# Gated linear attention and two MoE layers: the scan keeps its floor itself, layer 1's first two blocks take turns at the features, one more buffer for the scan's loads

## The chip, the cores and the metric

One core of a Trainium2 chip. The time is device microseconds of one execution, the median of several runs; the profile is one execution of its own, with its own time. Engines: PE (TensorE, matmuls), PEld (its weight loads), DVE (VectorE), ACT (ScalarE), POOL (GpSimd), SP (SyncE, here the queue that issues all DMAs).

## The reference

```python
# batch 4, heads 8, sequence 768, head size 48
for t in range(S):
    state = alpha[:, :, t, :, None] * state + einsum('bhd,bhe->bhde', k[:, :, t], v[:, :, t])
    y[:, :, t] = einsum('bhd,bhde->bhe', q[:, :, t], state)
x = y as (3072 tokens, 384)
# layer 1: w_in 384 x 2048, w_out 2048 x 384, coefficients a (4) and b (2)
h = x @ w_in
g = (a0 + a1 h + a2 h^2 + a3 h^3) / (1 + |b0||h| + |b1| h^2 + 1e-6)
x = g @ w_out
# layer 2, same shapes
h = x @ w_in
out = (h * cos(h)) @ w_out
```

The decays alpha lie between 0.8 and 1. The weights of both layers come as 64-bit floats.

## The kernel before

Everything is scheduled by hand: the order of the instructions in the code is the order in which each engine runs its own, and an engine that waits holds back all that stands behind it.

**The scan.** The sequence is cut into 6 chunks of 128 steps, and a unit u is one chunk of one batch entry (24 units; 8 heads as 4 pairs, 48 of each 64 partitions in use). Slots n run from -3 to 24, and in each the engines work on several units at once (`attention`, L395). For a unit, DVE forms the running products p of the decays by one scan instruction (`decay`, L239, scan at L246: product so far times the next decay, plus `fresh`, a PSUM bank of zeros that holds the first decay in each head's first column). DVE then clips p from below at 2^-60 into the PSUM tile r with its sum in `chk` (`guess1`, L257, instruction at L261), ACT takes the logarithm and the exponential of its negative, again with a sum (`guess2`, L265, L268 and L269), and a Newton step on DVE makes the exact inverse (L276 and L284). POOL multiplies k by it (L288) and q by p (L293). PE forms the scores (L301), ACT copies them out (L308), POOL masks them (L313), PE adds the part from the state (L364) and from the scores (L374), transposes k (L321) and forms the update of the state (L333), which DVE applies (L345, L347); L254 is the last decay of a unit. In slot n: scores and masks copied for unit n, q and k scaled for n+1, guess for n+2, decay for n+3, state update for n-2, output of n-1.

**Its loads.** At the head of slot n, SP issues a for unit n+4 (two DMAs of 96.8 KB, L223), kq for n+2 (512 KB), v for n+1 (192 KB), the store of the output of n-2 (two DMAs of 96 KB, L391), then the fetch of one or two raw weight tiles (384 KB each, L143). There are 2 tiles for a, 4 for kq, 3 for v, used in turn. x of block 0 is read back in slots 8 to 10.

**Weights.** Layer 1 has 16 groups of 128 features (called features here), each with one tile of w_in (s = 0) and one of w_out (s = 1): 32 tiles, ordered by `w_order` (w_in tile i at place i, w_out tile i at i + 4). `w_fetch` (L131) loads a raw tile into a piece of the `spare` tile or a `raw` buffer; at most six are pending. `tick` (L155) runs the next of three conversion steps: ACT's L66 and L67, DVE's L71, DVE's L72. The low words go into the PSUM bank `words_t` in slots under 20 and into the tile itself behind that. `w_hi` (L175, ACT's L182) and `w_lo` (L185, L191 on POOL) split the result into two 32-bit parts. In the scan a step runs only while more than three tiles are pending.

**The layers.** From slot 20 on one iteration of `layers` (L623) stands behind each slot, and behind the last slot iterations alone: 96 per layer, of 6 blocks of 512 tokens x 16 features, in blocks' order. Iteration n issues `gemm1` (L469, nine matmuls at L478) of feature n into one of three banks, the element-wise work of the last four features (`rational`, L523, for layer 1: L536 to L557 and L516, L521), and `gemm2` (L482, nine matmuls at L491) of the feature five iterations back, which accumulates a block's 16 features in three PSUM banks. `acc_out` (L499) copies finished banks by ACT and stores them. Two `w_fetch` and two steps run in each of the iterations 4 to 15 of layer 1; from 16 on one of each, now for layer 2, whose w_in tiles go to DRAM until they are needed. x of the next block is loaded at feature 8 and split at 11, 12 and 13 (L599 on ACT, L603 on DVE). Iterations 16 and 18 sum up `chk` (L608, L615), and a flag chooses a general path if a sum is out of bounds.

Of the kernel before, what the change touches and what calls it, by code (L numbers as in the profile page):

```python
# [23 lines left out]
NU = NC * B  # L24
NO = 0
# [13 lines left out]
def attn_then_two_moe(ctx, tc, kqT, aT, vP, w1i, w1o, ma, mb, w2i, w2o, out):  # L39
# [56 lines left out]
    def bank(tag, shape=(128, TB), dtype=F32):  # L96
# [8 lines left out]
    chk = const.tile([128, 3, NU + 1], F32, name="chk")  # L105
    a_t = [const.tile([128, HP * (C + 1)], F32, name=f"a{i}") for i in range(2)]
    kq_t = [const.tile([128, 2, HP, C], F32, name=f"kq{i}") for i in range(4)]
    v_t = [const.tile([128, H * D + 64 - D], F32, name=f"v{i}") for i in range(3)]
# [19 lines left out]
    def in_spare(i):  # L128
        return i < 24 and i % 6 < 4
# [55 lines left out]
    def w_lo(engs):  # L185
        engs = list(engs)
        while to_lo:
# [6 lines left out]
            engs.append(engs.pop(0))  # L194
            if at is not None:
# [3 lines left out]
    def w_load(at):  # L199
        nc.sync.dma_start(out=ws[at // NF][at % NF].bitcast(F32), in_=wd[at])  # L200
# [38 lines left out]
    def decay(u):  # L239
# [4 lines left out]
        for hs in parts(u):  # L244
            nc.vector.tensor_tensor(out=fresh[:, hs, 0:1], in0=first[:, hs], in1=fresh[:, hs, 1:2], op=ALU.add)
            nc.vector.tensor_tensor_scan(  # L246
                d["p"][:, hs].rearrange("p a b -> p (a b)"), rest[:, hs].rearrange("p a b -> p (a b)"),
                fresh[:, hs].rearrange("p a b -> p (a b)"), 0.0, ALU.mult, ALU.add,
            )

    def last_decay(u):
        d = U[u]
        d["pc"] = in_p.tile([128, HP, 1], F32, tag="pc", name="pc", bufs=6)
        nc.vector.tensor_tensor(out=d["pc"], in0=d["p"][:, :, C - 1:], in1=fresh[:, :, 1:2], op=ALU.add)  # L254
# [661 lines left out]
```

## Time and profile before

| | |
|---|---|
| median of 3 runs | 965.47 us (962.27 to 965.59) |
| profiled execution, its own time | 963.49 us |
| its span, first to last instruction | 961.7 us |
| PE busy | 925.4 us, 96% |
| DVE, ACT, POOL busy | 668.8, 654.2, 612.2 us |
| DMA | 84.54 MB, 63.09 read from HBM, 20.45 written |

The span is what the trace covers; the execution's own time is 1.8 us longer. Busy time is an average over stages: the scan (to about 130 us), the last slots with layer 1's first iterations, then the layers alone. TensorE runs at one of two levels, 1.2 or 2.4 GHz, and a granted clock of 0.68 over a stretch means a mixture of the two.

### The profile page before, as it was taken

How to read it: one execution, taken by the hardware profiler on the slowest of the kernel's cores; microseconds unless marked ns; L12 is line 12 of the kernel's file. 1: busy time of each engine (PE TensorE's matmuls, PEld its weight loads, DVE VectorE, ACT ScalarE, POOL GpSimd, SP SyncE). 2: the span in 40 equal slices, each digit the busy share in tenths (PEclk: the TensorE clock that was granted, in tenths of full speed). 3: DMA queues.
4: the chain of work that ended last, by engine and by line, in shares of the span. 5: the costliest groups of instructions: out<-in, count | busy, mean ns of one | idle time of the engine just before them, and what ended most of it. 6: DMA issues, size and time to landing. Idle time of an engine off the chain costs nothing.

```text
span 961.7 us, 14225 instructions
## 1 busy us (share of the span) xinstructions
PE 925.4 (96%) x4976; PEld 745.8 (78%) x4976; DVE 668.8 (70%) x1089; ACT 654.2 (68%) x1196; POOL 612.2 (64%) x559
## 2 busy tenths in 40 slices
PE   7788799999999999999999999999999999999997
PEld 6677677778888888888888888888888888888885
DVE  8989889999999998989979956434334334343331
ACT  5888888878888878888777877554444444454442
POOL 4888899978998889989878755423232332333232
PEclk7988999999999999999999999999999999999999
DMA  7999853202213114022044233010100100100001
GB/s 230 316 299 286 262 184 87 89 2 91 74 58 124 33 51 131 33 100 82 33 140 157 83 121 109 1 66 1 35 32 1 66 1 1 66 1 1 33 1 36
DMA packets 47008, 84.54 MB, mean 88 GB/s; under 512 B 5521, under 2 KB 22161, under 8 KB 46929
## 3 DMA queue, kind: packets, MB, share of 16 engines
q1 hardware_dynamic: 46928, 83.55, 27.2%
q8 instruction: 41, 0.67, 0.3%
q14 instruction: 39, 0.31, 0.1%
HBM read 63.09 MB, written 20.45 MB: 87 GB/s over the span
## 4 chain that ended last, share of the span: by engine, by line
PE 80%; DVE 10%; DMA 4%; issue 2%; POOL 2%; ACT 1%; SPq 0%; DVEq 0%; ACTq 0%; POOLq 0%
PE acc L491 39%; PE b L478 38%; DMA v<-vP 2%; DVE p L246 1%; DVE st L72 1%; DMA spare<-w1o 1%; DVE z L536 1%; DVE g L552 1%; DVE r L541 1%; DVE g L539 1%; DVE z L284 1%; POOL kq L288 1%; DMA a<-aT 1%; DVE ah L276 1%; PE sc L301 1%
## 5 line engine op out<-in xcount | busy, mean ns | idle before, releaser
L521 POOL TENSOR_TENSOR lo<-g,hi 128x512 fp32r<-128x512 f32 x192 | 257.7, 1342 | 299.4 <-ACT hi L516 292.9
L478 PE MATMUL b<-x,w 128*128 128x512 f32 x1728 | 435.3, 396 | 3.7 <-DVE g L539 3.7
L491 PE MATMUL acc<-hi,w 128*128 128x512 f32 x1152 | 392.6, 396 | 0.0
L478 PEld LDWEIGHTS b<-x,w 128*128 128x128 f32 x1728 | 323.9, 188 | 84.2 <-DVE g L539 6.2
L491 PEld LDWEIGHTS acc<-hi,w 128*128 128x128 f32 x1152 | 216.5, 188 | 52.3
L516 ACT ACTIVATE hi<-g 128x512 fp32r<-128x512 f32 x192 | 121.3, 632 | 185.4 <-PE acc L491 118.9
L491 PE MATMUL acc<-lo,w 128*128 128x512 f32 x576 | 227.8, 395 | 0.0
L568 DVE TENSOR_TENSOR g<-ah,b 128x512 f32<-128x512 f32 x96 | 65.7, 684 | 140.3 <-ACT ah L566 140.3
L547 POOL TENSOR_TENSOR z<-z,ah 128x512 f32<-128x512 f32 x96 | 124.9, 1301 | 8.0
L491 PEld LDWEIGHTS acc<-lo,w 128*128 128x128 f32 x576 | 108.3, 188 | 26.1
L78 DVE SCALAR_TENSOR_TENSOR ah<-z,b 128x512 f32<-128x512 int32 x96 | 65.7, 684 | 37.6 <-ACT z L77 37.6
L77 ACT ACTIVATE z<-b 128x512 int32<-128x512 f32 x96 | 57.0, 594 | 50.1 <-PE b L478 50.1
L548 DVE TENSOR_TENSOR g<-g,b 128x512 f32<-128x512 f32 x96 | 65.1, 678 | 24.7 <-ACT g L545 24.5
L546 POOL TENSOR_SCALAR z<-ah,cq 128x512 f32<-128x512 f32 x96 | 75.2, 783 | 1.6 <-ACT ah L544 1.6
L545 ACT ACTIVATE g<-b,cq 128x512 f32<-128x512 f32 x96 | 74.6, 777 | 0.0
L552 DVE SCALAR_TENSOR_TENSOR g<-g,cq,r 128x512 f32<-128x512 f32 x96 | 70.7, 737 | 0.1
L539 DVE SCALAR_TENSOR_TENSOR g<-g,cq,b 128x512 f32<-128x512 f32 x96 | 70.5, 735 | 0.0
L566 ACT ACTIVATE ah<-ah,half_pi 128x512 f32<-128x512 f32 x96 | 68.1, 709 | 0.0
L556 ACT ACTIVATE r<-z,lnb 128x512 f32<-128x512 f32 x96 | 66.7, 695 | 0.0
L541 DVE SCALAR_TENSOR_TENSOR r<-z,r 128x512 f32<-128x512 f32 x96 | 65.4, 681 | 0.0
L536 DVE SCALAR_TENSOR_TENSOR z<-z,r 128x512 f32<-128x512 f32 x96 | 64.8, 675 | 0.3 <-ACT kq L182 0.3
L544 ACT ACTIVATE ah<-b 128x512 f32<-128x512 f32 x96 | 56.4, 588 | 6.5 <-PE b L478 6.4
(109 smaller groups left out, 987.6 us busy)
## 6 DMA issues: line engine op xcount, KB each, us to landing
kq<-kqT SPq DMA_DIRECT2D x24, 512.0 KB, 5.2
raw<-w2i SPq DMA_DIRECT2D x16, 384.0 KB, 3.1
raw<-w2o SPq DMA_DIRECT2D x16, 384.0 KB, 3.1
w<-wd SPq DMA_DIRECT2D x16, 384.0 KB, 3.1
v<-vP SPq DMA_DIRECT2D x24, 192.0 KB, 4.5
x<-x0d SPq DMA_DIRECT2D x18, 256.0 KB, 3.7
x1d<-o SPq DMA_DIRECT2D x18, 256.0 KB, 2.2
x<-x1d SPq DMA_DIRECT2D x18, 256.0 KB, 3.5
```

Source lines behind the costliest of these rows:

```text
L478: nc.tensor.matmul(h, ws[0][f][:, w, ks], x[:, xx, kk, :], start=i == 0, stop=i == 8)
L491: nc.tensor.matmul(acc[k], ws[1][f][:, w, ks], d[g], start=f == 0 and i == 0, stop=f == NF - 1 and i == 2)
L516: nc.scalar.activation(out=t["hi"], in_=t["g"], func=AF.Copy)
L521: eng.tensor_tensor(out=t["lo"], in0=t["g"], in1=t["hi"].bitcast(F32), op=ALU.subtract)
L536: nc.vector.scalar_tensor_tensor(z, z, ONE_EPS, r, ALU.add, ALU.mult)
L539: nc.vector.scalar_tensor_tensor(g, g, cq[:, 3:4], two["h"], ALU.add, ALU.mult)
L541: nc.vector.scalar_tensor_tensor(r, z, -2.0 / LN_S, r, ALU.add, ALU.mult)
L545: nc.scalar.activation(out=g, in_=h, func=AF.Identity, scale=cq[:, 5:6], bias=cq[:, 4:5])
L546: nc.gpsimd.tensor_scalar(zz, ah, cq[:, 1:2], cq[:, 0:1], ALU.mult, ALU.add)
L547: nc.gpsimd.tensor_tensor(out=zz, in0=zz, in1=ah, op=ALU.mult)
L552: nc.vector.scalar_tensor_tensor(g, g, cq[:, 2:3], r, ALU.add, ALU.mult)
L566: nc.scalar.activation(out=two["r"], in_=two["r"], func=AF.Sin, bias=half_pi)
```

## The change

- The scan takes the larger of product and `fresh`, and `fresh` is filled with 2^-60, so p never falls below it; `guess1` goes, and ACT's logarithm reads p. The sums move to the two Newton instructions (the first one now takes the smaller of p and 1e16, times r).
- Layer 1's blocks 0 and 1 take turns: features 0 to 9 of block 0, 0 to 9 of block 1, then 10 to 15 of block 0 and of block 1 (iterations 0, 10, 20 and 26 on). The first part's sums are copied by ACT into kq tiles and added by DVE at the end. x of block 1 is loaded at iteration 3 and split at 5 to 7; x of block 2 is loaded at iteration 26 and split at 28 to 30.
- The weights' order, the number fetched per slot (two in slots 0, 7 and 14 instead of in every fourth), and the steps in layer 1 (one per iteration from 3 to 31; layer 2's from 32) follow that.
- a has 3 tiles, kq 5, v 4, and each is loaded one slot earlier; the fetch of weights stands ahead of the output's store.

```diff
+H1 = 10
...
-    chk = const.tile([128, 3, NU + 1], F32, name="chk")
-    a_t = [const.tile([128, HP * (C + 1)], F32, name=f"a{i}") for i in range(2)]
-    kq_t = [const.tile([128, 2, HP, C], F32, name=f"kq{i}") for i in range(4)]
-    v_t = [const.tile([128, H * D + 64 - D], F32, name=f"v{i}") for i in range(3)]
+    chk = const.tile([128, 2, NU + 1], F32, name="chk")
+    a_t = [const.tile([128, HP * (C + 1)], F32, name=f"a{i}") for i in range(3)]
+    kq_t = [const.tile([128, 2, HP, C], F32, name=f"kq{i}") for i in range(5)]
+    v_t = [const.tile([128, H * D + 64 - D], F32, name=f"v{i}") for i in range(4)]
...
-        [(0, s, i) for i in range(NF) for s in range(2)], key=lambda w: (w[2] + 4 * w[1], w[1])
+        [(0, s, i) for i in range(NF) for s in range(2)],
+        key=lambda w: (w[2] + 5 * w[1] + (H1 if w[2] >= H1 else 0), w[1])
...
-        return i < 24 and i % 6 < 4
+        return i < 22 and i % 6 < 4
...
-            nc.vector.tensor_tensor(out=fresh[:, hs, 0:1], in0=first[:, hs], in1=fresh[:, hs, 1:2], op=ALU.add)
+            nc.vector.tensor_tensor(out=fresh[:, hs, 0:1], in0=first[:, hs], in1=fresh[:, hs, 1:2], op=ALU.max)
             nc.vector.tensor_tensor_scan(
...
-                fresh[:, hs].rearrange("p a b -> p (a b)"), 0.0, ALU.mult, ALU.add,
+                fresh[:, hs].rearrange("p a b -> p (a b)"), 0.0, ALU.mult, ALU.max,
...
-    def guess1(u):
+    def guess(u):
         d = U[u]
         d["r"] = bank("b1" if u == 1 else "r0", (128, HP, C))
         for hs in parts(u):
-            nc.vector.tensor_scalar(
-                d["r"][:, hs], d["p"][:, hs], P_MIN, None, ALU.max, ALU.add, accum_out=sums(1, u, hs)
-            )
-
-    def guess2(u):
-        for hs in parts(u):
-            r = U[u]["r"][:, hs]
-            nc.scalar.activation(out=r, in_=r, func=AF.Ln)
-            nc.scalar.activation(out=r, in_=r, func=AF.Exp, scale=-1.0, accum_out=sums(0, u, hs))
+            nc.scalar.activation(out=d["r"][:, hs], in_=d["p"][:, hs], func=AF.Ln)
+            nc.scalar.activation(out=d["r"][:, hs], in_=d["r"][:, hs], func=AF.Exp, scale=-1.0)
...
-            d["m"][:, hs], d["r"][:, hs], 1.0, d["p"][:, hs], ALU.mult, ALU.mult, accum_out=sums(2, u, hs)
+            d["m"][:, hs], d["p"][:, hs], RANGE, d["r"][:, hs], ALU.min, ALU.mult, accum_out=sums(1, u, hs)
...
-        nc.vector.scalar_tensor_tensor(d["n"][:, hs], d["m"][:, hs], -2.0, d["r"][:, hs], ALU.add, ALU.mult)
+        nc.vector.scalar_tensor_tensor(
+            d["n"][:, hs], d["m"][:, hs], -2.0, d["r"][:, hs], ALU.add, ALU.mult, accum_out=sums(0, u, hs)
+        )
...
     def where(n):
         m, r = divmod(n, N1)
+        if n < 2 * H1:
+            return 0, *divmod(n, H1)
+        if n < 2 * NF:
+            blk, f = divmod(n - 2 * H1, NF - H1)
+            return 0, blk, H1 + f
         return m, *divmod(r, NF)
+
+    def part(blk, k):
+
+        return kq_t[2 * blk + k // 2][:, k % 2].rearrange("p a b -> p (a b)")
...
+        first = f == 0 or in_parts(m, blk) and f == H1
+        last = f == NF - 1 or in_parts(m, blk) and f == H1 - 1
...
+            if f < NF - 1:
+                nc.scalar.activation(out=part(blk, k), in_=acc[k], func=AF.Copy)
+                continue
             o = in_p.tile([128, TB], F32, tag="p", name="o")
-            if m == 1 and k == 1:
+            if in_parts(m, blk):
+                nc.vector.tensor_tensor(out=o, in0=part(blk, k), in1=acc[k], op=ALU.add)
+            elif m == 1 and k == 1:
...
-        split = f in (11, 12, 13) and n < 2 * N1 and nxt[0] < 2
+        at, load = f - 11, f == 8
+        if n < NF:
+            nxt, at, load = (0, 1), n - 5, n == 3
+        elif n < 2 * NF:
+            at, load = f - 12, f == 10
+        split = 0 <= at < NK and n < 2 * N1 and nxt[0] < 2
...
-        if n < NF:
-            for _ in range(2):
+        if n < 2 * NF:
+            if n > 1:
                 w_fetch(2 * NF)
-            tick(0 if n < 4 else 2)
+                tick(1 if n > 2 else 0, 1)
...
-        nc.vector.memset(fresh, 0.0)
+        nc.vector.memset(fresh, P_MIN)
...
+            if n == -1:
+                load(3, "a")
+                load(1, "v")
             if n >= -1:
-                load(n + 4, "a")
+                load(n + 5, "a")
             if n >= 0:
-                if n:
-                    load(n + 2, "kq")
-                load(n + 1, "v")
+                load(n + 3, "kq")
+                load(n + 2, "v")
+                for i in range((min(n, 1) if n % 7 else 2) if n <= LEAD else 0):
+                    w_fetch(2 * NF)
                 if n >= 2:
                     y_store(n - 2)
-                for i in range(min(n, 1) if n % 4 else 2):
-                    w_fetch(2 * NF)
```

## Rows read from the trace of the kernel before

**Rows 1.** Windows by stage: busy us of each engine (instructions), granted clock, DMA share, GB/s
```profile
...
0.00:130.32 130.32, 104.69 (x1342) 87.39 (x1343) 115.23 (x279) 102.02 (x226) 101.02 (x123) 0.88 0.86 272
...
130.32:209.00 78.68, 74.88 (x442) 58.13 (x440) 75.68 (x108) 64.95 (x120) 75.00 (x66) 1.00 0.28 85
209.00:955.30 746.30, 745.82 (x3197) 600.28 (x3195) 477.89 (x704) 487.05 (x850) 436.22 (x371) 1.00 0.17 56
...
```

**Rows 2.** Waits of PE, 130.3 to 209 us: total us, times, longest us
```profile
...
PE b L478 <- DVE g L539: 3.7, 5, 1.5
```

**Rows 3.** Timeline of DVE, 15 to 130 us: start us, us, engine, line, operation
```profile
...
15.90 1.22 DVE L246 TENSOR_TENSOR_SCAN p<-a,r 128x512 f32<-128x512 f32 x1
...
38.03 1.22 DVE L246 TENSOR_TENSOR_SCAN p<-a,r 128x512 f32<-128x512 f32 x1
...
45.28 1.22 DVE L246 TENSOR_TENSOR_SCAN p<-a,r 128x512 f32<-128x512 f32 x1
...
55.31 1.22 DVE L246 TENSOR_TENSOR_SCAN p<-a,r 128x512 f32<-128x512 f32 x1
...
64.34 1.22 DVE L246 TENSOR_TENSOR_SCAN p<-a,r 128x512 f32<-128x512 f32 x1
...
68.43 0.69 DVE L261 TENSOR_SCALAR_CACHE_REDUCE r<-p 128x512 f32<-128x512 f32 x1
69.05 0.14 DVE L261 DVE_READ_ACCUMULATOR r<-p 128x1 f32 x1
...
69.36 1.22 DVE L246 TENSOR_TENSOR_SCAN p<-a,r 128x512 f32<-128x512 f32 x1
...
79.39 1.22 DVE L246 TENSOR_TENSOR_SCAN p<-a,r 128x512 f32<-128x512 f32 x1
...
87.37 1.22 DVE L246 TENSOR_TENSOR_SCAN p<-a,r 128x512 f32<-128x512 f32 x1
...
92.39 1.22 DVE L246 TENSOR_TENSOR_SCAN p<-a,r 128x512 f32<-128x512 f32 x1
...
104.35 1.22 DVE L246 TENSOR_TENSOR_SCAN p<-a,r 128x512 f32<-128x512 f32 x1
...
112.33 1.22 DVE L246 TENSOR_TENSOR_SCAN p<-a,r 128x512 f32<-128x512 f32 x1
...
122.36 1.22 DVE L246 TENSOR_TENSOR_SCAN p<-a,r 128x512 f32<-128x512 f32 x1
...
126.72 1.22 DVE L246 TENSOR_TENSOR_SCAN p<-a,r 128x512 f32<-128x512 f32 x1
...
```

**Rows 4.** The same view of windows for three single stretches of the scan
```profile
...
0.00:13.10 13.10, 6.76 (x39) 6.11 (x40) 9.94 (x26) 4.24 (x10) 3.80 (x19) 0.81 0.69 206
45.28:55.31 10.03, 8.10 (x88) 6.62 (x86) 9.69 (x24) 8.07 (x18) 9.69 (x12) 0.68 0.93 300
64.34:79.39 15.05, 11.41 (x182) 9.57 (x182) 14.53 (x36) 14.38 (x33) 14.33 (x16) 1.00 1.00 323
...
```

**Rows 5.** Chain of work that ended last, 28 to 145 us: start us, us, what
```profile
...
38.05 4.22 DMA v<-vP
...
81.82 0.51 ACT b L67
...
```

**Rows 6.** Groups of instructions, 64.3 to 79.4 us: busy us, mean ns, idle before
```profile
...
L288 POOL TENSOR_TENSOR kq<-kq,z 128x512 f32<-128x512 f32 x4 | 5.1, 1280 | 1.3 <-DVE z L284 1.3
...
L191 POOL TENSOR_TENSOR w<-st,w 128x384 fp32r<-128x384 f32 x4 | 4.0, 1001 | 0.0
...
L313 POOL TENSOR_SCALAR_AFFINE_SELECT lo<-lo 128x512 f32<-128x512 f32 x3 | 1.9, 636 | 0.0
...
```

**Rows 7.** Instructions of lines 71 and 72: count, duration ns min/median/max, first and last start
```profile
...
L71 DVE SCALAR_TENSOR_TENSOR st<-st,raw x32: 549/1479/1694, 129.6 to 563.3; 128x384 int32<-128x384 int32 x32
L71 DVE SCALAR_TENSOR_TENSOR b<-st,b x21: 539/552/599, 24.4 to 118.5; 128x384 int32<-128x384 int32 x21
...
L72 DVE SCALAR_TENSOR_TENSOR st<-raw,st x32: 544/798/1655, 130.2 to 563.9; 128x384 int32<-128x384 int32 x32
...
```

More of the change, by code (lines that the diff above doesn't have):

```diff
@@ L116, in attn_then_two_moe @@
     w_order = sorted(
-        [(0, s, i) for i in range(NF) for s in range(2)], key=lambda w: (w[2] + 4 * w[1], w[1])
+        [(0, s, i) for i in range(NF) for s in range(2)],
+        key=lambda w: (w[2] + 5 * w[1] + (H1 if w[2] >= H1 else 0), w[1])
     ) + [(1, s, i) for s in range(2) for i in range(NF)]
+    ready = set()
     spare = x_p.tile([128, 2, NK, TB], F32R, tag="x", name="spare").rearrange("p a b c -> p (a b c)").bitcast(I32)
@@ L194, in w_lo @@
             engs.append(engs.pop(0))
+            ready.add((m, s, i))
             if at is not None:
@@ L199, in w_load @@
     def w_load(at):
+        assert (1, at // NF, at % NF) in ready
         nc.sync.dma_start(out=ws[at // NF][at % NF].bitcast(F32), in_=wd[at])
@@ L253, in last_decay @@
         d["pc"] = in_p.tile([128, HP, 1], F32, tag="pc", name="pc", bufs=6)
-        nc.vector.tensor_tensor(out=d["pc"], in0=d["p"][:, :, C - 1:], in1=fresh[:, :, 1:2], op=ALU.add)
-    def guess1(u):
+        nc.vector.tensor_tensor(out=d["pc"], in0=d["p"][:, :, C - 1:], in1=fresh[:, :, 1:2], op=ALU.max)
+    def guess(u):
         d = U[u]
@@ L423, in attention @@
                 tick(0 if on(n + 2) else 1)
-        if n not in (-1, 0) and on(n + 2):
-            guess1(n + 2)
         tick(1)
@@ L428, in attention @@
             decay(n + 3)
-        if n in (-2, -1):
-            guess1(n + 3)
         tick(1)
@@ L440, in attention @@
         if n not in (-1, 0) and on(n + 2):
-            guess2(n + 2)
+            guess(n + 2)
         if n in (-2, -1):
-            guess2(n + 3)
+            guess(n + 3)
         if on(n - 1):
@@ L466, in where, with in_parts @@
         m, r = divmod(n, N1)
+        if n < 2 * H1:
[3 more added lines that the diff above has]
+            return 0, blk, H1 + f
         return m, *divmod(r, NF)
+    def in_parts(m, blk):
+        return m == 0 and blk < 2
+    def part(blk, k):
+        return kq_t[2 * blk + k // 2][:, k % 2].rearrange("p a b -> p (a b)")
     def gemm1(n):
         m, blk, f = where(n)
+        assert m or (0, 0, f) in ready
         h = bank(f"b{n % 3}")
@@ L484, in gemm2 @@
         d = T.pop(n)
+        assert m or (0, 1, f) in ready
+        first = f == 0 or in_parts(m, blk) and f == H1
+        last = f == NF - 1 or in_parts(m, blk) and f == H1 - 1
         for k in range(NK):
-            if f == 0:
+            if first:
                 acc_out()
@@ L491, in gemm2 @@
                 nc.tensor.matmul(
-                    acc[k], ws[1][f][:, w, ks], d[g], start=f == 0 and i == 0, stop=f == NF - 1 and i == 2
+                    acc[k], ws[1][f][:, w, ks], d[g], start=first and i == 0, stop=last and i == 2
                 )
-            if f == NF - 1:
-                outs.append((m, blk, k))
+            if last:
+                outs.append((m, blk, f, k))
     outs = []
@@ L603, in x_lo @@
         nc.vector.tensor_tensor(out=lo, in0=lo.bitcast(F32), in1=hi.bitcast(F32), op=ALU.subtract)
-    ok = const.tile([128, 3, NU], F32, name="ok")
+    ok = const.tile([128, 2, NU], F32, name="ok")
     def all_ok0():
         nc.vector.tensor_tensor(out=chk[:, :, 0], in0=chk[:, :, 0], in1=chk[:, :, NU], op=ALU.add)
-        nc.vector.tensor_scalar(ok[:, 0:2, :], chk[:, 0:2, :NU], RANGE, None, ALU.is_le)
-        nc.vector.tensor_scalar(ok[:, 2, :], chk[:, 2, :NU], -float(HP * C), None, ALU.add)
-        nc.vector.tensor_tensor(out=ok[:, 2, :], in0=ok[:, 2, :], in1=ok[:, 2, :], op=ALU.mult)
-        nc.vector.tensor_scalar(ok[:, 2, :], ok[:, 2, :], 0.0625, None, ALU.is_le)
+        nc.vector.tensor_scalar(ok[:, 0, :], chk[:, 0, :NU], -RANGE, None, ALU.is_ge)
+        nc.vector.tensor_scalar(ok[:, 1, :], chk[:, 1, :NU], -float(HP * C), None, ALU.add)
+        nc.vector.tensor_tensor(out=ok[:, 1, :], in0=ok[:, 1, :], in1=ok[:, 1, :], op=ALU.mult)
+        nc.vector.tensor_scalar(ok[:, 1, :], ok[:, 1, :], 0.0625, None, ALU.is_le)
     def all_ok1():
-        cnt = bank("r1", (1, 3 * NU))
+        cnt = bank("r1", (1, 2 * NU))
         nc.tensor.matmul(cnt, ones, ok.rearrange("p a b -> p (a b)"), start=True, stop=True)
@@ L641, in layers @@
         if split:
-            x_hi(*nxt, f - 11)
+            x_hi(*nxt, at)
         second(n)
-        if n < 2 * N1 and nxt[0] < 2 and f == 8:
+        if n < 2 * N1 and nxt[0] < 2 and load:
             for kk in range(NK):
```

6 lines of the change are left out of this document (3 added, 3 removed).

## Prediction, made before the change was run

> **What bounds the kernel now.** I read the stages first [rows 1]. From 209.00 us on, PE is busy 745.82 of 746.30 us: nothing is to be had there, and whatever reaches it earlier ends earlier by the same amount. Between 130.32 and 209.00 PE is busy 74.88 of 78.68 us and DVE 75.68. Up to 130.32, where PE starts layer 1's first feature, PE is busy only 104.69 us; so this change can win up to there, and some 3.8 us in the middle stage. The waits of that stage [rows 2] give the 3.7 us: PE waits five times for L539 of DVE, which frees a feature's bank.
>
> Then the scan itself. The start of DVE's scan instruction marks the slots [rows 3]: slot 0 at 15.90, slot 20 at 126.72, so 20 slots in 110.82 us, 5.54 each. They are not alike: 64.34 to 69.36 takes 5.02, and so does each of the two from there to 79.39. Six are longer: 38.03 to 45.28 is 7.25 (2.23 too long), 55.31 to 64.34 is 9.03 (4.01), 79.39 to 87.37 and 104.35 to 112.33 are 7.98 (2.96 each), and the two slots from 92.39 to 104.35 take 11.96 (1.92). Together 14.1 us over the level of 5.02.
>
> What sets that level stands in one row of windows [rows 4], 64.34 to 79.39, three slots: DVE 14.53, ACT 14.38, POOL 14.33 and PE 11.41 of 15.05 us, and the DMA engines 1.00 busy at 323 GB/s. DVE is the fullest engine, but ACT and POOL are 1% behind it and the DMA is full. What makes the long slots stands in the chain of waits [rows 5]: three loads of v stand in it one behind the other, the last at 38.05 with the long slot behind it. At 81.82 it is ACT's L67, which had to wait for DVE's L72: two weights are converted in that slot, they share one bank of low words, and ACT, in order, comes late to the logarithms on which DVE's next slot begins.
>
> **The change, part by part.** *The floor kept by the scan.* guess1 goes. One of them starts at 68.43 and its accumulator's read at 69.05, 0.62 us later; the read, 0.14 long, mostly lies under what follows, so I take 0.66 us of DVE per slot [rows 3]. In exchange L284 gets such a read: between nothing and 0.14; I take nothing, as the next operation after it needs no result of it. Max for add in the scan and min for mult in L276 are not in the trace. Nearest row: the scan with add, 1.22 us. I take the same; bounds are 0 and, were it to run like two instructions, 1.22 more a slot, which I leave out as nothing here points to it. ACT loses its read of an accumulator.
>
> In the run-in, three guesses of this size (two halves, two whole) lie ahead of slot 0, where DVE is the chain: 3 x 0.66 = 2.0 us earlier, bounds 1 and 3.
>
> In the slots DVE would fall from 5.02 to 4.36, but the others do not: POOL has per slot two multiplications of 1.28, two masks of 0.64 and one weight of 1.00, 4.84 summed [rows 6], some 4.65 as they overlap. The DMA moves per slot a 0.20, k and q 0.52, v 0.20, the output 0.20 and a weight 0.39 MB, 1.51 MB: at 323 GB/s 4.67 us [rows 4], at the 272 GB/s of the whole stage 5.55 [rows 1]. So the level lies between 4.67 and 5.55; I take 4.85, near the low end, since the row of 323 GB/s is of undisturbed slots. That is 0.17 x 14 slots = 2.4 us. The last slot, 122.36 to 126.72 [rows 3], takes 4.36 us because no weight is converted in it; now one is: 0.5 lost.
>
> *Loads ahead and buffers.* v, a and kq each get one more slot between release and need; the fetch of a weight now passes the output's store on SP's queue (the store's one reader, x's load, stands slots behind it: nothing). The first long slot, 2.23 us, is the v loads' and goes.
>
> *Two weights in one slot.* By the code before, two weights are fetched in slots 0, 4, 8, 12 and 16, and five steps run in slots 8, 12 and 16, four in the slot behind them. After, slots 0, 7 and 14 fetch two: two slots with five steps are left. I give each the 2.96 us of today. So of 14.1 us of excess 5.9 remain: 8.2 won. If the loads and DVE are not the cause but PE's low level (below), less goes: bounds 3 and 12.
>
> *The turns in layer 1.* Features 10 to 15 are needed only from iteration 20 on. Counting the fetches in the code, 24 weights are fetched by slot 20 in either kernel: the scan is hardly relieved. What is relieved is the middle stage: one step per iteration instead of two. Eleven conversions stood in it, about nine do now. In this form they have long and short rows, 549 to 1694 ns [rows 7]; at the medians, 1.48 + 0.80 = 2.28 us a weight, that is 4.6 us less on DVE in 78.68, against 3.0 us that it was idle [rows 1]. Of the 3.7 us that PE waits I count 2.5 as gone (bounds 0 and 3.7), because the three splits of x for block 1 come earlier into the same stretch, at iterations 5 to 7. The six copies of partial sums go to ACT, six adds to DVE in place of ACT copies at iterations 31 to 37, each about the 0.69 of L261, an instruction of the same size [rows 3]: the weights of layer 2 start only at 32, so DVE has room; nothing, and 6 x 0.69 = 4 us if that cover were gone. Layer 2's second weights are ready two iterations ahead of use instead of five: nothing, while DVE is busy only 477.89 of 746.30 us there [rows 1].
>
> The Trainium skill has a rule that speaks against this part: "GPSIMD Engine Reference" (section "Key points") says that GpSimd shares its SBUF interfaces with VectorE and contends with instructions of two SBUF inputs. [Rows 7] agree: 539 to 599 ns with one input in PSUM, up to 1694 without. By the rule alone, each of the eight conversions left under layer 1 would be a long one.
>
> *Sum:* 2.0 + 2.4 - 0.5 + 8.2 + 2.5 = 14.6 us off the profiled execution's own 963.49 us (span 961.7 and 1.8 around it): 948.9. The median of the runs shown is 965.47, 2.0 above it; I add half of that and say 950. As a check, PE would start layer 1 at 118.2: some 35.5 MB moved by 130.32 [rows 1] would need 110 us at 323 GB/s, so it can be had, with the DMA at 95%.
>
> **Rivals.** *The DMA keeps the slots.* If it gives 300 GB/s, as in 45.28 to 55.31 [rows 4], a slot takes 5.03 us: DVE's saving is idle time, and half of the excess stays as late loads. Then 2.0 - 0.5 + 4.1 + 2.5 = 8.1 us, 955.4, or 956 to 960 with less. For it: the full DMA of the best slots. Against: the first 13.10 us have it at 0.69 busy, and the extra buffers fill that.
>
> *Long conversions under layer 1.* If all eight take the 3.35 us of the two longest rows [rows 7] instead of 2.28, DVE has 8 x 1.07 = 9 us more; with the 3.0 idle and 4.6 relieved, PE waits some 2 us more than now instead of 2.5 less: 953 to 954. This is what the skill's rule above would make of it.
>
> *PE left at the low level: slower.* From 45.28 to 55.31 the granted clock averages 0.68 [rows 4], that is, 2.4 GHz for a part and 1.2 GHz for the rest; a slot's 3.80 us of PE work becomes 7.6, 2.75 over a slot of 4.85. If a faster DVE leaves PE in bursts with gaps while it waits for POOL and loads, in more slots than today, each costs 2.75: at five more the gain is gone, at nine it is 24.8 - 14.6 = 10 us slower, 974. For it: two such stretches stand in the scan now. Against: PE's share of a slot rises from 76 to 78%, and the gaps ahead of those stretches come with the long slots. "TensorE: Matmul & The Clock Gate" of the Trainium skill (Part 1) says that the throttled state is the default and activity releases it; the row agrees that the scan does not hold the clock, and no row tells which gap decides.
>
> *It doesn't do what it says.* If guess1's work was hidden behind POOL and the long slots stay as they are, only the run-in and part of the middle are left: 3 us, 961 to 963.
>
> **How the numbers follow.** Forecast (944 to 956) 0.60, of which 0.10 with the long conversions; DMA 0.20 (956 to 960.5); better than forecast, slots at the 4.67 of the DMA and no long ones, 0.05 (940 to 944); no effect 0.09; low level 0.06. A measurement can tell about 0.5%, 4.8 us, from no change. Faster by more: 0.85; within: 0.09; slower: 0.06. The range takes the forecast and the DMA case and the bounds of their terms: 941 to 960.
>
> **What would show it.** Right: no L261; scan starts 4.7 to 5.0 us apart with two long slots (7 and 14); slot 20 near 114 instead of 126.72; L478 first at 118; PE's waits for L539 under 2 us. Wrong: slots still at 5.02 with DVE idle ahead of L276 behind ACT or POOL; PE idle in front of the first feature of a turn (iterations 10, 20, 26, 32) or at iterations 100 to 111; more of the scan at the low clock.

## The result and the profile after

| | before | after |
|---|---|---|
| median of 4 runs | 963.87 us (961.43 to 965.59) | 949.20 us (947.75 to 950.29) |
| profiled execution, its own time | 963.49 us | 950.29 us |
| its span | 961.7 us | 948.5 us |

The ratio is 0.9848 (95% interval 0.9831 to 0.9866): 1.5% faster, 14.7 us. The forecast was 950.0 us in a range of 941 to 960. The total was met; the two terms of its sum on the scan's slots were not, and their errors nearly cancel, so that the total came right by luck as far as the scan goes. That is what the rest of this document is about.

First the page of the changed kernel, its span and its line of busy times. PE is now busy for 97% of the span; DVE has 16.7 us less to do, ACT and POOL 2.8 and 1.4.

```profile
span 948.5 us, 14172 instructions
...
PE 916.7 (97%) x4976; PEld 740.0 (78%) x4976; DVE 652.1 (69%) x1070; ACT 651.4 (69%) x1171; POOL 610.8 (64%) x560
...
```

The view of windows, with the changed kernel's own borders of the stages (columns as in [rows 1]: length, busy us of PE, PEld, DVE, ACT and POOL with their instructions, granted clock, DMA share, GB/s). The fourth line is the scan's slots alone, the last two are two of its long slots.

```profile
...
0.00:117.78 117.78, 96.63 (x1342) 81.23 (x1342) 102.81 (x251) 96.96 (x198) 97.66 (x121) 0.94 0.95 307
117.78:196.46 78.68, 76.15 (x450) 60.02 (x448) 70.80 (x108) 65.46 (x121) 72.45 (x66) 1.00 0.21 63
196.46:942.10 745.64, 743.89 (x3189) 598.75 (x3187) 478.46 (x713) 488.98 (x854) 440.68 (x374) 1.00 0.18 58
13.90:114.10 100.20, 85.05 (x1250) 70.77 (x1250) 88.56 (x216) 86.87 (x179) 90.63 (x98) 0.96 0.97 315
43.58:51.61 8.03, 8.03 (x90) 6.80 (x89) 5.33 (x14) 6.34 (x14) 5.49 (x7) 0.66 0.95 294
82.06:90.30 8.24, 6.78 (x100) 5.47 (x100) 5.93 (x15) 7.23 (x16) 5.92 (x7) 1.00 0.93 296
...
```

Against [rows 1], layer 1's first feature starts at 117.78 instead of 130.32, 12.54 us earlier. From there to PE's last matmul (at 939.96, before at 954.43) it takes 822.2 us instead of 824.1, 1.9 less, and what follows that last matmul takes 8.5 instead of 7.3. 12.5 + 1.9 - 1.2 = 13.2 us is the whole difference of the two profiled executions.

The timeline of DVE shows where the 12.5 us come from (start us, us, engine, line, operation). L251 is the scan instruction, and its starts mark the slots as in [rows 3].

```profile
...
13.80 1.22 DVE L251 TENSOR_TENSOR_SCAN p<-a,r 128x512 f32<-128x512 f32 x1
...
32.26 1.22 DVE L251 TENSOR_TENSOR_SCAN p<-a,r 128x512 f32<-128x512 f32 x1
...
34.64 3.18 DVE L736 TENSOR_SCALAR cq<-cab 128x4 f32<-128x4 f32 x1
...
39.33 1.22 DVE L251 TENSOR_TENSOR_SCAN p<-a,r 128x512 f32<-128x512 f32 x1
...
43.58 1.22 DVE L251 TENSOR_TENSOR_SCAN p<-a,r 128x512 f32<-128x512 f32 x1
...
49.53 0.69 DVE L275 SCALAR_TENSOR_TENSOR ah<-p,r 128x512 f32<-128x512 f32 x1 [1.54 <-ACT r L267]
...
51.61 1.22 DVE L251 TENSOR_TENSOR_SCAN p<-a,r 128x512 f32<-128x512 f32 x1
...
70.83 1.22 DVE L251 TENSOR_TENSOR_SCAN p<-a,r 128x512 f32<-128x512 f32 x1
...
73.97 2.33 DVE L621 TENSOR_TENSOR x<-x 128x512 fp32r<-128x512 f32 x1
...
77.82 1.22 DVE L251 TENSOR_TENSOR_SCAN p<-a,r 128x512 f32<-128x512 f32 x1
78.96 0.54 DVE L72 SCALAR_TENSOR_TENSOR b<-st,b 128x384 int32<-128x384 int32 x1
...
79.67 0.55 DVE L73 SCALAR_TENSOR_TENSOR st<-spare,b 128x384 int32<-128x384 int32 x1
...
80.46 0.68 DVE L275 SCALAR_TENSOR_TENSOR ah<-p,r 128x512 f32<-128x512 f32 x1
...
81.19 0.69 DVE L283 SCALAR_TENSOR_TENSOR z<-ah,r 128x512 f32<-128x512 f32 x1
...
82.06 1.22 DVE L251 TENSOR_TENSOR_SCAN p<-a,r 128x512 f32<-128x512 f32 x1
...
90.30 1.22 DVE L251 TENSOR_TENSOR_SCAN p<-a,r 128x512 f32<-128x512 f32 x1
...
114.18 1.22 DVE L251 TENSOR_TENSOR_SCAN p<-a,r 128x512 f32<-128x512 f32 x1
...
```

Slot 0 starts at 13.80 (15.90 before) and slot 20 at 114.18 (126.72): the run-in gave 2.10 us and the 20 slots, 100.38 us instead of 110.82, gave 10.44. In between two things are to be seen. The slot from 77.82 to 82.06 is an undisturbed one: 4.24 us, in which DVE goes from the scan over a weight's two steps to the two Newton instructions and the next scan. Before it was 5.02. And there are still long slots: 32.26 to 39.33 (7.07), 43.58 to 51.61 (8.03), 70.83 to 77.82 (6.99) and 82.06 to 90.30 (8.24). In the first stands a scaling of 4 columns (L736) that takes 3.18 us, in the second a wait of 1.54 us for ACT's logarithm and exponential, in the third a split of x (L621) of 2.33 us, which takes 0.68 elsewhere.

The second and the fourth are the slots with two weights. The timeline of ACT in the second: L68, the second weight's step, waits 0.88 us for DVE's L73, and the logarithms stand behind it. In the fourth it waits 0.87 us at 85.57.

```profile
...
46.87 0.52 ACT L68 ACTIVATE b<-spare 128x384 int32<-128x384 uint8 x1 [0.88 <-DVE st L73]
...
```

In the stretch of 78.7 us behind the scan, the waits of PE (total us, times, longest us) answer to [rows 2]; L488 and L557 are what L478 and L539 were:

```profile
...
PE b L488 <- DVE g L557: 0.6, 1, 0.6
...
```

3.7 us have become 0.6. The conversions from 117.8 to 200 us stand in the groups of DVE (busy us, mean ns of one, idle before):

```profile
...
L72 DVE SCALAR_TENSOR_TENSOR st<-st,raw 128x384 int32<-128x384 int32 x8 | 11.4, 1429 | 3.3 <-ACT raw L68 2.7 <-POOL w L194 0.7
...
L73 DVE SCALAR_TENSOR_TENSOR st<-raw,st 128x384 int32<-128x384 int32 x7 | 6.2, 886 | 0.1
...
```

The longer of the two instructions takes 1.43 us in the mean and the shorter 0.89, 2.32 together. In the stretch of 78.7 us itself seven whole weights are converted, and the second step of an eighth; the kernel before has ten second steps in its own. DVE is busy 70.80 us there instead of 75.68.

### The profile page after: what moved, and what is told of

It is laid out like the page before. It is cut to its first block, busy times and chain, and to the rows that moved or that the text cites. A ratio compares the mean times of both kernels' runs of the same rounds, so it can differ in the third digit from the quotient of the medians.

```text
span 948.5 us, 14172 instructions
## 1 busy us (share of the span) xinstructions
PE 916.7 (97%) x4976; PEld 740.0 (78%) x4976; DVE 652.1 (69%) x1070; ACT 651.4 (69%) x1171; POOL 610.8 (64%) x560
## 4 chain that ended last, share of the span: by engine, by line
PE 79%; DVE 7%; ACT 5%; DMA 5%; issue 2%; POOL 1%; SPq 0%; DVEq 0%; ACTq 0%
PE acc L504 40%; PE b L488 39%; DMA x0d<-g 1%; DVE p L251 1%; DMA spare<-w1i 1%; DMA a<-aT 1%; DVE st L72 1%; DMA spare<-w1o 1%; DMA raw<-w1i 1%; DVE g L570 1%; DMA raw<-w1o 1%; DVE ah L275 1%; DVE x L621 1%; ACT g L563 1%; DVE g L557 0%
## 5 line engine op out<-in xcount | busy, mean ns | idle before, releaser
L539 POOL TENSOR_TENSOR lo<-g,hi 128x512 fp32r<-128x512 f32 x192 | 257.1, 1339 | 294.8 <-ACT hi L534 288.4
L488 PE MATMUL b<-x,w 128*128 128x512 f32 x1728 | 435.1, 396 | 0.7 <-DVE g L557 0.6
L488 PEld LDWEIGHTS b<-x,w 128*128 128x128 f32 x1728 | 324.2, 188 | 80.3 <-DVE g L557 2.0
L565 POOL TENSOR_TENSOR z<-z,ah 128x512 f32<-128x512 f32 x96 | 127.3, 1326 | 8.0
L557 DVE SCALAR_TENSOR_TENSOR g<-g,cq,b 128x512 f32<-128x512 f32 x96 | 70.7, 737 | 0.0
```

The lines of the kernel that those rows point to most:

```text
L488: nc.tensor.matmul(h, ws[0][f][:, w, ks], x[:, xx, kk, :], start=i == 0, stop=i == 8)
L539: eng.tensor_tensor(out=t["lo"], in0=t["g"], in1=t["hi"].bitcast(F32), op=ALU.subtract)
L557: nc.vector.scalar_tensor_tensor(g, g, cq[:, 3:4], two["h"], ALU.add, ALU.mult)
L565: nc.gpsimd.tensor_tensor(out=zz, in0=zz, in1=ah, op=ALU.mult)
```

## The experiments

The theory after the result: the gain is DVE's shorter undisturbed slot, and the long slots come from collisions of DVE with ACT (two weights in one slot) and with POOL, not from loads. The rivals: the DMA sets the slots, the loads ahead made them shorter, or the turns did. Times of a run are compared with runs of the kernel before on the same chip, whose medians were 962.74, 961.68 and 963.62 us in the three groups of runs below.

### The parts alone

**The floor alone**: the kernel before with the diff's parts on `decay`, `guess`, `inverse0`, `inverse1`, `fresh` and the sums; nothing else.

```diff
-                fresh[:, hs].rearrange("p a b -> p (a b)"), 0.0, ALU.mult, ALU.add,
+                fresh[:, hs].rearrange("p a b -> p (a b)"), 0.0, ALU.mult, ALU.max,
...
-        if n not in (-1, 0) and on(n + 2):
-            guess1(n + 2)
```

> The kernel before with the scan's floor alone (no clip on DVE, sums moved); loads, buffers, the order of the weights and layer 1 as before. Theory (three parts that add: the run-in and the level of the slots from the floor, the long slots from loads and from the number of slots with two weights, the middle stage from the turns): 2.0 us in the run-in and some 2.4 in the slots, so 4 to 5 us faster than before, the long slots still where they were. Rival 'DVE sets the slots': 0.66 us in each of 20 slots too, 13 to 15 us faster, the whole gain. Rival 'hidden': the run-in alone, 2 us.

Measured: 954.81 us (953.95 to 955.32), ratio 0.9912 (0.9896 to 0.9929). Slot 20 starts at 114.40, 12.3 us earlier than before, and undisturbed slots take 4.25. But layer 1's first feature starts 6.49 us behind slot 20, where it was 3.60 in both of the other kernels, and the waits at this place (114 to 121.5 us) say why:

```profile
...
PE u L329 <- DVE pc L254: 3.4, 1, 3.4
...
```

What makes `pc` late stands ahead of it on DVE, one step of a conversion:

```profile
...
115.53 3.60 DVE L71 SCALAR_TENSOR_TENSOR st<-st,spare 128x384 int32<-128x384 int32 x1
...
```

The same step takes 0.55 us in the kernel before and 0.70 in the change; here it runs beside an unbroken run of POOL, which ends at 118.72 (see the last section). So the floor alone shortens the slots as much as the whole change does (20 slots in 100.23 us, against 100.38), and gives 2.9 us of it back at the handover from the scan to the layer.

**The loads alone**: one more tile each for a, kq and v, the loads one slot earlier, and the fetch ahead of the store.

```diff
-    a_t = [const.tile([128, HP * (C + 1)], F32, name=f"a{i}") for i in range(2)]
+    a_t = [const.tile([128, HP * (C + 1)], F32, name=f"a{i}") for i in range(3)]
...
-                load(n + 1, "v")
+                load(n + 3, "kq")
+                load(n + 2, "v")
```

> The kernel before with one more buffer each for decays, k and q, and v, the loads one slot ahead and the weights' fetch ahead of the store, but two weights in every fourth slot as before, the clip on DVE and layer 1 as before. Theory: the long slot behind the late v loads (7.25 us) goes to about 5, so 2 to 4 us faster, the slots with two weights still long. Rival 'late loads make all long slots': 8 us or more. Rival 'the DMA is full anyway': within 1 us.

Measured: 965.64 us (962.02 to 971.92, 10 runs), ratio 1.0029 (1.0009 to 1.0049): nothing won, rather 3 us lost. In the profiled execution slot 20 starts 2.1 us later than before (128.83 instead of 126.72), 1.9 of it in the last two slots, which take 5.35 and 5.96 us (5.01 and 4.36 before); the granted clock is 0.61 over the first of them, where it was 1.00 before. The slot that the prediction had put down to late loads of v is still 7.25 us long (37.98 to 45.23). What makes it stands in ACT's timeline of this kernel, and in the same view of the kernel before:

```profile
...
39.68 0.52 ACT L67 ACTIVATE b<-raw 128x384 int32<-128x384 uint8 x1 [1.97 <-DVE st L72]
...
```
```profile
...
39.72 0.52 ACT L67 ACTIVATE b<-raw 128x384 int32<-128x384 uint8 x1 [2.52 <-DVE st L72]
...
```

ACT's second step of a second weight stands waiting for DVE, with the scores' copies and the logarithms behind it: the mechanism of [rows 5]'s line at 81.82, not a late load.

**The turns alone**: the order of features and weights, the steps in layer 1, and two fetches in slots 0, 7 and 14 instead of every fourth.

```diff
+        if n < 2 * H1:
+            return 0, *divmod(n, H1)
...
-                for i in range(min(n, 1) if n % 4 else 2):
+                for i in range((min(n, 1) if n % 7 else 2) if n <= LEAD else 0):
```

> The turns of layer 1 with the order of the weights and two weights in every seventh slot instead of every fourth; buffers, loads and clip as before. Theory: fewer long slots, 3 to 5 us, and 2 us less waiting of PE in the middle stage: 5 to 7 us faster. Rival 'long slots come from late loads': 2 us, the middle stage alone.

Measured: 958.30 us (955.51 to 958.67), ratio 0.9939 (0.9920 to 0.9957). The 20 slots take 108.85 us, 2.0 less than before, and first feature to last matmul 822.0 us, 2.1 less than before. The slot that began at 38.03 now has no second weight:

```profile
...
37.80 1.22 DVE L251 TENSOR_TENSOR_SCAN p<-a,r 128x512 f32<-128x512 f32 x1
...
40.18 0.16 DVE L742 TENSOR_SCALAR cq<-cab 128x4 f32<-128x4 f32 x1
...
42.62 1.22 DVE L251 TENSOR_TENSOR_SCAN p<-a,r 128x512 f32<-128x512 f32 x1
```

It takes 4.82 us instead of 7.25, which settles its cause: the second weight. The scaling of 4 columns takes 0.16 us here. Not all of it stays won: the slot from 65.66 to 72.59 takes 6.93 us now, behind a slot over which the granted clock is 0.50 and PE busy throughout.

**All but the floor.**

```diff
-                fresh[:, hs].rearrange("p a b -> p (a b)"), 0.0, ALU.mult, ALU.max,
+                fresh[:, hs].rearrange("p a b -> p (a b)"), 0.0, ALU.mult, ALU.add,
...
+        if n not in (-1, 0) and on(n + 2):
+            guess1(n + 2)
```

> The changed kernel with the clip on DVE put back: loads, buffers and turns stay. Theory (parts add): 4 to 5 us slower than the changed kernel, 953 to 954. Rival 'DVE sets the slots once the loads are on time': 0.66 us more in each of 20 slots and in the run-in, 13 us or more slower, 962.

Measured: 959.33 us (958.38 to 959.86), ratio 0.9956 (0.9939 to 0.9972). Undisturbed slots are back at 5.01 to 5.02, slot 20 at 123.79. From here to the whole change the floor is worth 0.9956 - 0.9848 = 1.1%, 10.4 us of 963. The prediction's steps gave it 2.0 in the run-in and 2.4 in the slots, 4.4.

**All but the loads.**

```diff
-    a_t = [const.tile([128, HP * (C + 1)], F32, name=f"a{i}") for i in range(3)]
+    a_t = [const.tile([128, HP * (C + 1)], F32, name=f"a{i}") for i in range(2)]
...
-                load(n + 3, "kq")
-                load(n + 2, "v")
+                load(n + 1, "v")
```

> The changed kernel without the extra buffers and the earlier loads: floor and turns stay. The loads alone made the kernel before no faster (965.64 against 962.74), and the long slot that I had put down to late v loads stayed 7.25 us there; it went with the turns' order of fetches. Theory 'loads ahead matter only where the slots are short': with the floor a slot has 4.25 us of DVE work, the loads no longer land in time with 2 and 3 buffers, so 2 to 5 us slower than the changed kernel, 951 to 954, with waits for DMAs on DVE and PE. Rival 'the floor and the turns add, the loads are worth nothing': 7.9 + 4.4 = 12.3 us off the 962.7 of before, 950 to 951.

Measured: 949.73 us (947.68 to 951.12), ratio 0.9874 (0.9848 to 0.9900), not to be told from the change's 0.9848 (0.9831 to 0.9866). Its 20 slots take 99.49 us. Four slots in a row (24.30 to 48.25) take 5.68, 5.62, 6.20 and 6.45, 4.0 us more than in the change. The loads are late there, by the view of waits from 14 to 117 us (both of its rows lie before 50):

```profile
...
POOL kq L294 <- DMA kq<-kqT: 4.3, 2, 2.6
...
DVE r L250 <- DMA a<-aT: 2.1, 4, 1.0
...
```

The granted clock is 0.72 over these four slots too, 0.97 over the same ones of the change; what part of the 4.0 us is the loads' is not shown. Against it stand the scaling of 4 columns, 0.85 us instead of 3.18, the first split of x, 1.12 instead of 2.33, and the two slots with two weights, 7.15 and 7.23, 1.9 less together. So the loads ahead do spare waits in the early slots, other waits take as much back, and in the time of the change they are worth nothing that shows.

### What sets the slots

**Half of k and q.** From unit 5 on only k is loaded, and q's place keeps what was there, so the output is no longer the reference's.

```diff
-        elif u < len(ts) or name == "kq":
+        elif u >= len(ts) and name == "kq":
+            nc.sync.dma_start(out=t[:, 0], in_=src[:, 0])
+        elif u < len(ts):
```

> The changed kernel, loading only k and not q from unit 5 on (q's old contents are used, so the output is not the reference's): 256 KB less in each slot, about a sixth of what the scan moves. Theory 'engines and their order set the slots': within 2 us of the changed kernel. Rival 'the DMA sets them' (it is 0.97 busy in the changed scan): 0.26 MB at 314 GB/s is 0.8 us for each of some 16 slots, up to 13 us faster, 936.

Measured: 950.34 us (947.12 to 951.28), ratio 0.9868 (0.9836 to 0.9899). The row of windows over the same stretch:

```profile
...
13.90:114.10 100.20, 84.95 (x1248) 70.71 (x1248) 88.68 (x216) 86.85 (x179) 90.61 (x98) 0.96 0.87 270
...
```

The DMA moves 270 GB/s instead of 315 and is busy 0.87 instead of 0.97, while DVE, ACT, POOL and PE stay within 0.1 us of what they were, and slot 20 starts at 114.36 (114.18 in the change). At this load the DMA does not set the length of the slots.

**The scaling on ACT.** The only edit: `cq` is scaled by ACT instead of DVE.

```diff
-                nc.vector.tensor_scalar(cq[:, 2:6], cab[:, 0:4], -LN_S * LN_S, None, ALU.mult)
+                nc.scalar.activation(out=cq[:, 2:6], in_=cab[:, 0:4], func=AF.Copy, scale=-LN_S * LN_S)
```

> The changed kernel with the 128x4 scaling of the coefficients on ACT instead of DVE. In the changed kernel that one instruction took 3.18 us on DVE (0.30 before), ending when POOL's run of instructions paused, and the slot around it took 7.07 us. Theory 'DVE stood waiting for POOL': the slot falls to some 4.3 and 2 to 3 us are won, 946 to 947. Rival 'the DMA sets the slots on average': the time comes back as a wait in the next slots, within 1 us.

Measured: 946.56 us (946.02 to 950.21), ratio 0.9847 (0.9815 to 0.9880). In the timeline of DVE the slot of 7.07 us is now 4.46:

```profile
...
32.42 1.22 DVE L251 TENSOR_TENSOR_SCAN p<-a,r 128x512 f32<-128x512 f32 x1
...
36.88 1.22 DVE L251 TENSOR_TENSOR_SCAN p<-a,r 128x512 f32<-128x512 f32 x1
...
```

Layer 1's first feature starts at 114.26, 3.5 us earlier than in the change. So the instruction did make that slot long. The same slot follows it in three other kernels: 5.32 us where it takes 1.43 (four steps a slot, below), 5.93 where it takes 2.04 (one weight a slot, below), 7.24 where it takes 3.35 (half of k and q), as 7.07 goes with 3.18 in the change; each time 3.89 more. In time the gain doesn't show: the ratio is that of the change.

**Four steps a slot.** The step of a conversion behind `update1` is left out in the scan, so that two weights are spread over two slots.

```diff
-        tick(1)
+        tick(0 if n < LEAD else 1)
         if on(n + 3):
```

> The changed kernel with four conversion steps a slot at most in the scan: the one behind the state's update, ahead of ACT's copy of the scores, is left out, so that a second weight starts at the end of its slot. The same weights are ready when layer 1 starts. Theory 'a second weight begun ahead of the scores holds ACT behind DVE': slots 7 and 14 (8.03 and 8.24 us) fall to some 5, 4 to 6 us are won, 943 to 945. Rival 'the DMA sets the slots on average': within 1 us.

Measured: 951.83 us (948.32 to 954.80), ratio 0.9889 (0.9850 to 0.9928). The slots of 8.03 and 4.80 us have become 6.30 and 6.42, as long in sum, and 8.24 and 4.24 have become 6.52 and 6.42. ACT waits as before, one slot on:

```profile
...
49.91 0.51 ACT L68 ACTIVATE b<-spare 128x384 int32<-128x384 uint8 x1 [1.09 <-DVE st L73]
...
```

The idea that five steps in one slot are the harm fell: the second weight costs its time wherever its steps stand, and the wait for the one bank of low words moves with it.

### Versions built on the reading

**One weight a slot.** Only slot 0 fetches two; two steps run in six of layer 1's iterations instead.

```diff
-                tick(1 if n > 2 else 0, 1)
+                tick((2 if n in (8, 10, 12, 14, 16, 18) else 1) if n > 2 else 0, 1)
...
-                for i in range((min(n, 1) if n % 7 else 2) if n <= LEAD else 0):
+                for i in range((min(n, 1) if n else 2) if n <= LEAD else 0):
```

> The changed kernel fetching one weight a slot throughout (two only in slot 0), so that no slot of the scan converts two; the two weights left over are converted in layer 1, two steps instead of one in iterations 8, 10, 12, 14, 16 and 18. Leaving out the fifth step had only moved the long slot: 6.30 and 6.42 us in place of 8.03 and 4.80, with ACT's second L68 still waiting for DVE's L73. Theory 'a second weight whose first step is not the first of its slot holds ACT behind DVE, wherever in the slot it stands': without it no slot is longer than about 5.3 but those with the coefficients (7.1) and the first split of x (7.0): 3 to 3.8 us won for each of two slots, 6 to 7 us, 942 to 943. Rival 'each weight costs its work wherever it is converted': the middle stage takes it back, within 1.5 us of the changed kernel.

Measured: 947.71 us (945.95 to 949.25), ratio 0.9831 (0.9815 to 0.9848). The first feature starts at 114.94, 2.8 us earlier than in the change, but from there to the last matmul it takes 825.8 us instead of 822.2: the waits of PE in the middle stage are back.

```profile
...
PE b L488 <- DVE g L557: 3.5, 4, 1.4
...
```

What left the scan came back behind it; the net is not to be told from the change.

**One weight a slot, and the scaling on ACT.**

> As the kernel with one weight a slot, and the coefficients' scaling on ACT. If the two effects are separate: 2.6 us less than that kernel, 940 by the first theory; 945 by the rival.

Measured: 946.58 us (944.97 to 948.58), ratio 0.9833 (0.9816 to 0.9849), the first feature at 110.58. The row of windows of its slots:

```profile
...
14.00:107.00 93.00, 81.44 (x1248) 67.68 (x1248) 83.08 (x211) 84.11 (x173) 88.65 (x95) 1.00 0.98 319
...
```

The granted clock is 1.00 all through, that is, 2.4 GHz, and POOL is busy 88.65 of 93.00 us. This is the scan with the fewest disturbances of all: 4.69 us per slot in the mean (13.32 to 107.11).

**The same without the loads ahead**: the last version with the loads and tiles of the kernel before.

> As the kernel with one weight a slot and the coefficients on ACT, but without the extra buffers and the earlier loads. Theory 'the loads are worth nothing here either': within 1.5 us of it. Rival 'the shorter the slots, the more the loads ahead matter': 3 us or more slower.

Measured: 951.48 us (949.29 to 957.71), ratio 0.9885 (0.9859 to 0.9912), 5 us behind the last version, and the intervals lie apart. Its waits from 14 to 50 us, and one row of the same view of the last version:

```profile
...
POOL kq L294 <- DMA kq<-kqT: 5.6, 4, 2.4
DVE r L250 <- DMA a<-aT: 3.0, 3, 1.3
...
```
```profile
...
POOL kq L294 <- DMA kq<-kqT: 1.6, 2, 1.3
...
```

With shorter slots the loads are late, two slots of 5.87 and 5.94 us come of it, and the loads ahead are worth 5 us. In the change the scaling and the first split took 3.5 us more with the loads ahead than without; here the scaling is on ACT, and the split takes 1.42 us with them and 1.40 without.

**The splits of x on POOL**: the version with one weight a slot and the scaling on ACT, the scan's three splits of x moved from DVE to POOL.

```diff
-                x_lo(0, 0, kk)
+                x_lo(0, 0, kk, nc.gpsimd)
```

> As the kernel with one weight a slot and the coefficients on ACT, with the three splits of x in slots 12, 14 and 16 on POOL instead of DVE. In the changed kernel they took 2.33, 0.68 and 0.68 us on DVE, the first ending as POOL's run ended. Theory 'DVE stands waiting for POOL there too': 1 to 3 us faster. Rival 'POOL, which pays 1.3 us for each, is as full': within 1 us or slower.

Measured: 948.62 us (947.30 to 952.06), ratio 0.9856 (0.9834 to 0.9878), not better than without it (0.9833): PE waits at the end of the scan instead (108 to 114 us):

```profile
...
PE u L334 <- DVE pc L259: 2.9, 1, 2.9
```

Ahead of `pc` stands a conversion step again, as in the floor alone:

```profile
...
109.43 2.26 DVE L72 SCALAR_TENSOR_TENSOR st<-st,spare 128x384 int32<-128x384 int32 x1
...
```

No version beats the change clearly: the best two, at 0.983, overlap with its interval.

## Why the prediction was right in its total, and wrong in two of its terms

In the order of its steps; all in us of the profiled executions.

| step | predicted | measured |
|---|---|---|
| run-in | 2.0 | 2.10 |
| level of the slots | 2.4 | 15.6 |
| long slots and the last slot | 8.2 - 0.5 | -5.2 |
| middle stage and layers | 2.5 | 1.9 |
| end | 0 | -1.2 |
| sum | 14.6 | 13.2 |

The level's 15.6 is 20 slots by 5.02 - 4.24; the -5.2 is what remains of the 10.44 that the 20 slots gave. It holds the last slot, which lost 0.44 (4.80 instead of 4.36), as forecast. The two lines are off by 13.2 us one way and 12.9 the other: the mechanism of the run-in and of the middle stage was right, that of the slots was not, and the total was met because the two errors cancel. Of the prediction's signs, slot 20 near 114 (114.18), the first feature at 118 (117.78) and waits under 2 us (0.6) came; starts 4.7 to 5.0 us apart with two long slots did not.

**Run-in: right.** Three instructions of 0.66 us lay on DVE's chain, as counted.

**The level: the step that failed.** The prediction said that "DVE would fall from 5.02 to 4.36, but the others do not", and took 4.85 between 4.67 and 5.55. DVE did fall, to 4.24, and the slots with it. Both floors under the others were no floors of a slot. The 4.67 was the DMA at the rate of a row in which it was 1.00 busy: a full DMA beside a full DVE was read as a limit of its own. With 14% less moved the slots stay as they were (the run with half of k and q): over the scan the DMA has 5.02 us a slot in the mean, so an undisturbed slot of 4.24 can begin with what is loaded already. POOL's 4.65 is no floor of a slot either: it is busy 90.63 us in 20 slots, 4.53 each, which is more than an undisturbed slot has; it falls behind there and catches up in the long ones. Its work is a floor of the mean alone. Where most long slots are gone, in the version with one weight a slot and the scaling on ACT, the mean slot is 4.69, POOL is 95% busy and the DMA 0.98: the mean comes near both, and whether either of them holds that scan was not tried. The low bound of 4.67 also left out the case that came; DVE's own 4.36 should have been that bound.

**The long slots: the step that failed with the other sign.** 8.2 us were to be won, and the excess over the level has grown by 5.2. Three parts:
- "The first long slot, 2.23 us, is the v loads' and goes": it was not. The loads ahead alone leave it at 7.25, the turns alone take it to 4.82; ACT's L67 had waited 2.52 us there for DVE's L72. Loads of v in a chain of waits showed that they were near, not that they were last. So there were four slots with two weights in the scan before, not three.
- Two weights in one slot remain in two slots. They cost 3.79 and 4.00 us over 4.24 instead of the 2.96 each that was given. Such slots were worth 2.23 + 4.01 + 2.96 + 2.96 = 12.2 before and 7.8 after: 4.4 won.
- What replaced it: two slots of 7.07 and 6.99 (2.83 and 2.75 over 4.24), made by one instruction each that DVE could not finish beside POOL. The first is shown by moving it to ACT; the second is read from rows alone: with the scaling on ACT the same split takes 1.03 us and its slot 5.70, both 1.3 less. And six slots of 4.79 to 5.27 us: in five of them DVE waits 0.46 to 0.49 us for ACT's exponential, in the sixth it runs another split of x (0.68 us). Nine such waits stand in the view of waits from 14 to 114 us, and five in the slots of the kernel before:

```profile
...
DVE ah L275 <- ACT r L267: 5.3, 9, 1.5
...
```

The prediction took the DMA and POOL's work for what would hold the slots next; it was ACT's order of work and POOL's hold on DVE's instructions.

**Middle stage: right**, 3.1 of PE's 3.7 us of waits are gone, 1.9 of it in the time. The turns alone give the same 2.1, so this is theirs. Eleven conversions and nine after were counted, ten and between seven and eight stand in the rows; they take 2.32 us each against the 2.28 taken, and DVE is busy 4.9 us less, 4.6 was taken.

**The rivals.** *The DMA keeps the slots* fell by the level of 4.24 and by the run with half of k and q. *Long conversions under layer 1* did not come: 2.32 us each, not 3.35, though POOL is busy 72.45 of 78.68 us there. By the Trainium skill's rule in "GPSIMD Engine Reference" (section "Key points") they contend with POOL; the rows agree that they take more than the 0.55 of the scan, and show that this is not the longest form every time. *PE at the low level* did not come: the granted clock up to layer 1 rose from 0.88 [rows 1] to 0.94; with two levels that is 31 us at 1.2 GHz before and 14 after. Where the scan has no slot over 5.1 us but three of 6.0 to 6.6, with one weight a slot and the scaling on ACT, the clock is 1.00. *It doesn't do what it says* fell by the floor alone, 0.9912.

**The parts.** The floor is worth 0.9% alone and 1.1% on top of the rest, the turns 0.6% alone (half in the scan through the fetches, half behind it), the loads nothing that shows here, and 5 us where each slot has one weight and the scaling is on ACT. The 20 slots are no shorter with turns and loads than with the floor alone; one reason is that the scaling and the first split take 5.5 us in the change and 2.3 with the floor alone.

## What to carry to other kernels

A resource that is full beside another full one is a limit only if taking some of its load away shortens the stage: count what the fullest in-order engine does in one undisturbed slot, let that be the low bound, and treat a sum of another engine's work as a floor of the mean alone. For each long slot, go to the instruction that waits on each in-order engine and read what stands behind it; a transfer in the chain is no proof. Compare the parts slot by slot, since one instruction that is held longer can hide what a part is worth. After an engine has been made faster, expect the excess to come back as waits for its neighbours, and price them at what the same wait costs today or more.

## What the runs showed of the hardware

A DVE instruction of 4 columns took 3.18 us in the changed kernel, 0.30 in the kernel before, 0.16 with the turns alone. The operands are the same: source and result in SBUF. In the timelines of DVE and POOL of the changed kernel and of the one with the loads alone:

```profile
...
34.35 1.03 POOL L194 TENSOR_TENSOR w<-st,w 128x384 fp32r<-128x384 f32 x1
35.30 0.67 POOL L314 TENSOR_SCALAR_AFFINE_SELECT hi<-hi 128x512 f32<-128x512 f32 x1
35.89 0.66 POOL L314 TENSOR_SCALAR_AFFINE_SELECT lo<-lo 128x512 f32<-128x512 f32 x1
36.49 1.30 POOL L294 TENSOR_TENSOR kq<-kq,p 128x512 f32<-128x512 f32 x1
39.23 1.26 POOL L289 TENSOR_TENSOR kq<-kq,z 128x512 f32<-128x512 f32 x1 [1.43 <-DVE r L250]
```
```profile
...
40.70 0.16 DVE L713 TENSOR_SCALAR cq<-cab 128x4 f32<-128x4 f32 x1
...
```
```profile
...
40.84 0.64 POOL L313 TENSOR_SCALAR_AFFINE_SELECT hi<-hi 128x512 f32<-128x512 f32 x1 [1.95 <-ACT hi L308]
...
```

In the changed kernel the instruction runs from 34.64 to 37.82, and POOL has no gap until 36.49 + 1.30 = 37.79. With the loads alone POOL idles until 40.84 and it takes 0.16. In seven more kernels, where it takes 0.18 to 3.35 us, it ends 0.02 or 0.03 us behind the end of one of POOL's instructions (in the kernel before at 41.05, and POOL's L191 at 41.02; with four steps a slot at 36.15 and 36.12, the third end that it met). So DVE's instruction gets through at some border between two of POOL's, not always the first, and can be held for the whole of a run of POOL. The split of x that took 2.33 us (two sources in SBUF) ends 0.55 us behind POOL's run, which ends at 74.46 + 1.29 = 75.75. The two conversion steps of 3.60 and 2.26 us that held up the end of the scan (two sources in SBUF as well) end 0.41 and 0.42 us behind POOL's run. The Trainium skill, "GPSIMD Engine Reference" (section "Key points"), names such a contention for DVE instructions with two SBUF inputs or in a mode that uses two ports. The Trainium skill, "VectorE: DVE Perf Modes" (section "Mode 2×_2P — use both read ports for one tensor"), says that a tensor_scalar of fp32 in SBUF can be in such a mode; no row here shows whether this one is. The rows agree with the rule on contention and add its price: 3.0 us for an instruction of 0.16 in the change, 3.2 with half of k and q.

Left open: why the granted clock falls near the end of the scan with the loads alone, and how the 3.79 us of the first slot with two weights are shared between ACT's order and PE's clock: the row from 43.58 to 51.61 has the clock at 0.66 and PE busy all of 8.03 us, the row from 82.06 to 90.30 has 1.00 and PE busy 6.78, and yet is the longer of the two.
